# An RWKV-6 attention and its squared-ReLU MoE: new orders, DMA transposes for 12 chunks, the first four chunks in pairs

## The chip, the cores and the metric

The kernel runs on one core of one Trainium2 chip. The metric is device time in microseconds (us). The time before is the median of 3 runs, 212.34 us (211.41 to 213.89).

## What is computed

A linear attention with a decaying state, over 4 batches, 8 heads, 768 steps and a head dimension of 48, followed by a layer of the form ReLU squared on 3072 tokens of 384 values with 2048 hidden values:

```python
for t in range(S):                      # per batch b and head h, S = 768
    kt, vt, rt, wt = k[:, :, t], v[:, :, t], r[:, :, t], w[:, :, t]
    cur = einsum('bhd,bhe->bhde', u[None] * kt, vt)
    y[:, :, t] = einsum('bhd,bhde->bhe', rt, state + cur)
    state = wt[:, :, :, None] * state + einsum('bhd,bhe->bhde', kt, vt)
x = y.transpose(0, 2, 1, 3).reshape(B * S, H * D)      # 3072 x 384
h = maximum(x @ w_in, 0)                               # w_in 384 x 2048
out = (h * h) @ w_out                                  # w_out 2048 x 384
```

Inputs and output are float32; products are made in bfloat16.

## The kernel before

**Attention by chunks.** The steps are cut into chunks of 128: 6 chunks in each of 4 batches, 24 chunks s = 0 to 23 (`NSTEP`). A chunk has its 128 time steps in the partitions, and all 8 heads side by side (384 values). Four loads bring it (w, r, k, v; `load_one`, L71). In memory each (head, step) row has 48 floats, so a load of 192 KB consists of 1024 pieces of 192 bytes. Then, in the names of the code:

- `lw_` takes the logarithm of w (ACT). `cum_` multiplies it on TensorE by a strict upper triangle and by a negative inclusive one (L180, L181), which gives the running sums before and, negated, after each step; four one-column products (L178) give the sum over the whole chunk. `exp_` takes the exponentials (ACT), and `rd_` multiplies r and k with them (VectorE). The result, `rdec`, has each head padded to 64 columns.
- `tr_` transposes `rdec` by 8 TensorE products and `rkt_` copies them out of PSUM (VectorE). From chunk 18 on (`DMA_FROM`), `dtr_` does both by a transposing DMA (L208).
- `p_` multiplies decayed k and r (L223), `pm_` masks the product with the triangle, in two halves (L229).
- `su_` forms k times v (L238), `ts_` adds the old state, and `sn_` decays it to the next state (GpSimd).
- `y_` forms masked product times v (L260) and, except in a batch's first chunk, adds r times old state (L268).
- The u part needs no TensorE: `ku_`, `qp_` (GpSimd), `q_` (sum over each head, VectorE) and `vq_` (times v, GpSimd). `ysb_` adds it to y (VectorE).
- `yt_` transposes y by three TensorE products and `xt_` copies it (ACT) into `xT`, the MoE's input. From chunk 18 on `dyt_` does it by a transposing DMA (L213).

**MoE by blocks.** A block is one or two chunks (`blocks`). `m1_` multiplies xT with w_in (L301) into PSUM, 512 values wide; `rl_` is the ReLU (ACT, L308), `gt_` the square (VectorE, L313), `m2_` the product with w_out (L320), `os_` the scaled copy out (ACT) and `store` the output DMA (L329). w_in and w_out come in four loads of 768 KB each and are cast to bfloat16 on ACT and VectorE (L110).

**The order.** Each operation is put in a plan with its engine, an assumed duration, a rank, and what it depends on. `make_order` runs a list schedule over it, and the result is the order of instructions in each engine's queue; all queues run in order. Where TensorE would idle ahead of the first `m2_`, multiplies of zeros are put in (`warm_`, L334). All DMAs are issued from SP's queue. The loads' order there is fixed:

```python
seq = [(0, x) for x in "wrkvu"] + [(1, x) for x in "wrkv"] + [(g, "i") for g in range(4)]
seq += [(2, x) for x in "wrkv"] + [(g, "o") for g in range(4)]
seq += [(s, x) for s in range(3, NSTEP) for x in "wrkv"]
```

A chunk's input buffers are seven deep (`A_IN`); stores have the first rank on SP, then `dtr_` and `dyt_`, then loads.

Of the kernel before, what the change touches and what calls it, by code (L numbers as in the profile page):

```python
# [9 lines left out]
FP32 = mybir.dt.float32  # L10
FP16 = mybir.dt.float16
# [4 lines left out]

@with_exitstack
def kernel(
# [12 lines left out]
    PSUM = bass.MemoryType.PSUM  # L31

# [9 lines left out]
    NSTEP = B * NCH  # L42
    GW = 512
    RS = 16.0
    A_IN = 7
    HOP = .2
    PACE = 0.0
    DMA_FROM = 18
    LAG = 3.5

    nc.scalar.preload_act_table_set("natural_log_exp_and_others")

    consts = ctx.enter_context(tc.tile_pool(name="consts", bufs=1))
    weights = ctx.enter_context(tc.tile_pool(name="weights", bufs=1))
    stage_pool = ctx.enter_context(tc.tile_pool(name="stage", bufs=8))
    a_in = ctx.enter_context(tc.tile_pool(name="a_in", bufs=A_IN))
    a_mid = ctx.enter_context(tc.tile_pool(name="a_mid", bufs=2))
    a_small = ctx.enter_context(tc.tile_pool(name="a_small", bufs=3))
    gt_pool = ctx.enter_context(tc.tile_pool(name="gt", bufs=3))
    relu_pool = ctx.enter_context(tc.tile_pool(name="relu", bufs=3))  # L60
    o_pool = ctx.enter_context(tc.tile_pool(name="moe_out", bufs=3))

    ps_cp = ctx.enter_context(tc.tile_pool(name="ps_cp", bufs=1, space=PSUM))
    ps_y_pool = ctx.enter_context(tc.tile_pool(name="ps_y", bufs=1, space=PSUM))
    ps_tr_pool = ctx.enter_context(tc.tile_pool(name="ps_tr", bufs=1, space=PSUM))
    ps_m1 = ctx.enter_context(tc.tile_pool(name="ps_m1", bufs=2, space=PSUM))
    ps_m2 = ctx.enter_context(tc.tile_pool(name="ps_m2", bufs=1, space=PSUM))


    def load_one(dst, src, b, c):  # L70
        nc.sync.dma_start(  # L71
            out=dst, in_=src[b, :, c * C:(c + 1) * C, :].rearrange("h c d -> c h d"))

    raw = {}

    def load_step(step, part):
        b, c = divmod(step, NCH)
        if part == "w":
            raw["w", step] = a_in.tile([C, H, D], FP32, name="w_raw")
            load_one(raw["w", step][:], w, b, c)  # L80
        elif part == "r":
            raw["rk", step] = a_in.tile([C, 2, H, D], FP32, name="rk_raw")
            load_one(raw["rk", step][:, 0], r, b, c)
        elif part == "k":
            load_one(raw["rk", step][:, 1], k, b, c)
        else:
            raw["v", step] = a_in.tile([C, H, D], FP32, name="v_raw")
            load_one(raw["v", step][:], v, b, c)

    wi_sb = weights.tile([C, KT, DFF], BF16)  # L90
    wo_sb = weights.tile([C, NT, DM], BF16)
    xT = weights.tile([C, KT, B * S], BF16)
    w_st = {}

    def load_wi(g):
        w_st["i", g] = stage_pool.tile([C, KT, GW], FP32, name="w_st")
        nc.sync.dma_start(  # L97
            out=w_st["i", g][:],
            in_=moe_w_in[:, g * GW:(g + 1) * GW].rearrange("(a p) f -> p a f", p=128))

    def load_wo(g):
        w_st["o", g] = stage_pool.tile([C, 4, DM], FP32, name="w_st")
        nc.sync.dma_start(
            out=w_st["o", g][:],
            in_=moe_w_out[g * 512:(g + 1) * 512, :].rearrange("(a p) d -> p a d", p=128))

    def cast(eng, kind, g, j):
        dst = wi_sb[:, :, g * GW:(g + 1) * GW] if kind == "i" else wo_sb[:, g * 4:(g + 1) * 4, :]
        copy = nc.scalar.copy if eng == "A" else nc.vector.tensor_copy
        copy(dst[:, j], w_st[kind, g][:, j])  # L110

    u_bc = consts.tile([C, H, D], FP32)

    def load_u():
        nc.sync.dma_start(
            out=u_bc[:],
            in_=bass.AP(tensor=u.tensor, offset=u.offset,
                        ap=[[0, C]] + [list(x) for x in u.ap]))


    tri_strict = consts.tile([C, C], BF16)
    make_upper_triangular(nc, tri_strict[:], val=1.0, diag=False)
    tri_incl_neg = consts.tile([C, C], BF16)
    make_upper_triangular(nc, tri_incl_neg[:], val=-1.0, diag=True)
    ident = consts.tile([C, C], BF16)
    make_identity(nc, ident[:])
    ones_col = consts.tile([C, 1], BF16)
    nc.vector.memset(ones_col[:], 1.0)

    warm = consts.tile([C, 512], BF16)  # L130
    nc.vector.memset(warm[:], 0.0)  # L131

    NLW = 3
    lw_bufs = []
    for i in range(NLW):
        t = consts.tile([C, H, DP], BF16, name=f"lw_buf{i}")
        nc.gpsimd.memset(t[:], 0.0)
        lw_bufs.append(t)
    NRD = 3
    rdec_bufs = []  # L140
    for i in range(NRD):
        t = consts.tile([C, 2, H, DP], BF16, name=f"rdec_buf{i}")
        nc.vector.memset(t[:], 0.0)
        rdec_bufs.append(t)


    tiles = {}

    def lw_(s):
        lw = tiles["lw", s] = lw_bufs[s % NLW]  # L150
        nc.scalar.activation(lw[:, :, 0:D], raw["w", s][:], AF.Ln)  # L151

    def v_(s):
        v_bf = tiles["v", s] = a_mid.tile([C, H, D], BF16, name="v_bf", bufs=3)
        nc.scalar.copy(v_bf[:], raw["v", s][:])  # L155

    def ku_(s):
        ku = tiles["ku", s] = a_mid.tile([C, H, D], FP32, name="ku")
        nc.gpsimd.tensor_mul(ku[:], raw["rk", s][:, 1], u_bc[:])  # L159

    def qp_(s):
        qp = tiles["qp", s] = a_mid.tile([C, H, D], FP32, name="qprod")
        nc.gpsimd.tensor_mul(qp[:], raw["rk", s][:, 0], tiles.pop(("ku", s))[:])  # L163

    def q_(s):
        q = tiles["q", s] = a_small.tile([C, H], FP32, name="q")
        nc.vector.reduce_sum(q[:], tiles.pop(("qp", s))[:], axis=AX.X)  # L167

    def vq_(s):
        vq = tiles["vq", s] = a_mid.tile([C, H, D], FP32, name="vq", bufs=3)  # L170
        nc.gpsimd.tensor_mul(vq[:], raw["v", s][:],  # L171
                             tiles.pop(("q", s))[:, :, None].to_broadcast([C, H, D]))

    def cum_(s):
        lw = tiles.pop(("lw", s))
        cs = tiles["cs", s] = ps_cp.tile([C, 2, 512], FP32, name="cp")
        for p in range(HP):
            nc.tensor.matmul(cs[:, 0, DM + p:DM + p + 1], lw[:, 2 * p:2 * p + 2, :],  # L178
                             ones_col[:], start=True, stop=True)
        nc.tensor.matmul(cs[:, 0, 0:DM], tri_strict[:], lw[:, :, 0:D], start=True, stop=True)  # L180
        nc.tensor.matmul(cs[:, 1, 0:DM], tri_incl_neg[:], lw[:, :, 0:D], start=True, stop=True)  # L181

    def exp_(s):
        cs = tiles["cs", s]
        a_c = tiles["a_c", s] = a_small.tile([C, HP], FP32, name="a_c")
        nc.scalar.activation(a_c[:], cs[:, 0, DM:DM + HP], AF.Exp)
        nc.scalar.activation(cs[:, :, 0:DM], cs[:, :, 0:DM], AF.Exp)  # L187

    def rd_(s):
        rdec = tiles["rdec", s] = rdec_bufs[s % NRD]  # L190
        nc.vector.tensor_mul(  # L191
            rdec[:, :, :, 0:D], raw["rk", s][:],
            tiles.pop(("cs", s))[:, :, 0:DM].rearrange("p a (h d) -> p a h d", h=H))

    def tr_(s):
        rdec = tiles["rdec", s]
        ps_tr = tiles["tr", s] = ps_tr_pool.tile([C, 2, HP, C], BF16, name="tr")
        for i in range(2):
            for p in range(HP):
                nc.tensor.transpose(ps_tr[:, i, p, :], rdec[:, i, 2 * p:2 * p + 2, :], ident[:])  # L200

    def rkt_(s):
        rkT = tiles["rkT", s] = a_mid.tile([C, 2, HP, C], BF16, name="rkT")
        nc.vector.tensor_copy(rkT[:], tiles.pop(("tr", s))[:])  # L204

    def dtr_(s):
        rkT = tiles["rkT", s] = a_mid.tile([C, 2, HP, C], BF16, name="rkT")
        nc.sync.dma_start_transpose(  # L208
            out=rkT[:].rearrange("p i a t -> p (i a) t"),
            in_=tiles["rdec", s][:].rearrange("t i h d -> t (i h d)"))  # L210

    def dyt_(s):
        nc.sync.dma_start_transpose(  # L213
            out=xT[:, :, s * C:(s + 1) * C],
            in_=tiles.pop(("ysb", s))[:].rearrange("p h d -> p (h d)"))

    def p_(s):
        rkT = tiles["rkT", s]
        ps_p = tiles["p", s] = ps_cp.tile([C, 2, 512], FP32, name="cp")
        for p in range(HP):  # L220
            for e in range(2):
                rows = slice(e * DP, (e + 1) * DP)
# [291 lines left out]
```

## Time and profile before

| what | value |
|---|---|
| median of 3 runs | 212.34 us |
| the profiled execution: time, span, mean TensorE clock granted | 213.79 us, 212.0 us, 0.992 |
| L301 (m1): 480 products of 256 columns, 192 of 128 | 77.2 us busy |
| L320 (m2): 384 products of 384 columns | 74.8 us busy |
| L334 (warm-up): 60 products of 512 columns | 16.8 us busy |
| ReLU, L308, 128 x 512 | 96 x 598 ns |
| square, L313, 128 x 512 | 96 x 562 ns (median 425) |
| masking, L229, 128 x 512 | 48 x 682 ns |
| exponential, L187, 128 x 768 | 24 x 797 ns |
| ku, qp, vq on GpSimd | 24 each, 1012, 1052, 889 ns |
| `sn_` on GpSimd, 128 x 192 | 20 x 552 ns |
| a chunk load of 192 KB, issue to landing | 4.2 us (3.0 to 11.2) |
| dtr, issue to landing | 6, 3.3 us (3.0 to 4.6) |
| dyt, issue to landing | 6, 2.3 us (2.3 to 2.6) |
| a store of 192 KB, issue to landing | 2.0 us (1.9 to 4.3) |
| DMA: 115984 packets of data, share of the 16 engines' span | 72.6% |

Five engines are listed: PE (TensorE's products), PEld (its weight loads, which lie beside the products), DVE (VectorE), ACT (ScalarE) and POOL (GpSimd). SP is the queue that issues DMAs. In the 40 slices each digit is the busy share in tenths; a slice is 5.3 us. A line in order of time gives start, length, engine, line, operation, output and input, and the number of instructions in it. TensorE's products overlap, so the mean duration of one is longer than the distance to the next.

### The profile page before, as it was taken

The page shows a single profiled execution, that of the slowest core. Times are in us where ns is not written, and L with a number is a line of the kernel's source. Part 1 is how long each engine was busy: PE and PEld are TensorE (multiplying, and loading weights), DVE is VectorE, ACT ScalarE, POOL GpSimd, SP SyncE. Part 2 cuts the span into 40 slices and gives each one's busy share as a digit, 9 for nine tenths or more (in the row PEclk, how much of TensorE's full clock was granted, in tenths as well). Part 3 has the DMA queues.
Part 4 walks back from the last instruction along what each step waited for, and adds up shares of the span by engine and source line. Part 5 has one row for each costly group of instructions (what it writes and reads, how often), then busy time and mean ns, then how long its engine had stood idle before and what let it go on. Part 6 is the DMA issues. An engine that isn't in the chain of part 4 may idle for free.

```text
span 212.0 us, 5530 instructions
## 1 busy us (share of the span) xinstructions
PE 194.2 (92%) x2162; PEld 138.1 (65%) x2166; DVE 147.3 (69%) x273; ACT 125.2 (59%) x249; POOL 83.5 (39%) x105
## 2 busy tenths in 40 slices
PE   7897997886999898989989999999999999999983
PEld 3354766554877665767767677777767777777751
DVE  3565795555799798979968999987786666533310
ACT  3353967644666667568477376787645753455530
POOL 5371320545655719747276376363712110000000
PEclk9999999999799999999999999999999999999999
DMA  7999899879975899599978978899444327111111
GB/s 129 202 324 340 200 383 219 170 160 192 181 152 117 174 163 195 107 200 167 178 166 160 204 165 159 155 205 150 101 107 108 62 63 108 56 40 37 39 46 68
DMA packets 116010, 32.61 MB, mean 154 GB/s; under 512 B 109200, under 2 KB 114448, under 8 KB 115984
## 3 DMA queue, kind: packets, MB, share of 16 engines
q1 hardware_dynamic: 115984, 32.25, 72.6%
q8 instruction: 17, 0.28, 0.6%
q14 instruction: 9, 0.07, 0.1%
HBM read 25.36 MB, written 4.72 MB: 142 GB/s over the span
## 4 chain that ended last, share of the span: by engine, by line
PE 44%; DMA 17%; SPq 12%; issue 8%; DVE 8%; POOL 5%; ACT 4%; DVEq 0%; POOLq 0%; ACTq 0%
PE m L320 18%; PE m L301 17%; SPq L71 9%; DMA v_raw<-in_v_dram 6%; DMA w_st<-in_moe_w_out_dram 4%; DMA w_raw<-in_w_dram 3%; DVE gt L313 3%; PE cp L223 2%; POOL qprod L163 2%; DMA rk_raw<-in_r_dram 2%; DVE pmT L229 2%; PE tr L200 2%; ACT o_sb L325 2%; DMA rk_raw<-in_k_dram 2%; SPq L97 1%
## 5 line engine op out<-in xcount | busy, mean ns | idle before, releaser
L301 PE MATMUL m<-xT,wi_sb 128*128 128x256 bf16 (+1 forms) x672 | 77.2, 260 | 3.6 <-ACT xT L286 2.5
L308 ACT ACTIVATE rl<-m 128x512 f16<-128x512 f32 x96 | 56.5, 598 | 39.9 <-PE m L301 39.0
L320 PE MATMUL m<-wo_sb,gt 128*128 128x384 bf16 x384 | 74.8, 326 | 1.8 <-ACT o_sb L325 0.8
L301 PEld LDWEIGHTS <-wi_sb 128*128 128x128 bf16 x672 | 59.0, 99 | 16.8 <-issue 4.7
L313 DVE TENSOR_TENSOR gt<-rl 128x512 bf16<-128x512 f16 x96 | 52.5, 562 | 19.7 <-ACT rl L308 19.5
L320 PEld LDWEIGHTS <-gt 128*128 128x128 bf16 x384 | 35.3, 98 | 20.7 <-DVE gt L313 1.5
L159 POOL TENSOR_TENSOR ku<-rk_raw,u_bc 128x384 f32<-128x384 f32 x24 | 24.3, 1012 | 45.7 <-DMA rk_raw<-in_k_dram 41.1
L229 DVE TENSOR_TENSOR pmT<-cp,tri_strict 128x512 bf16<-128x512 f32 x48 | 30.8, 682 | 4.6 <-PE cp L223 4.4
L191 DVE TENSOR_TENSOR rdec_buf<-rk_raw,cp 128x768 bf16<-128x768 f32 x24 | 22.8, 949 | 13.9 <-ACT cp L187 10.9
L171 POOL TENSOR_TENSOR vq<-v_raw,q 128x384 f32<-128x384 f32 x24 | 21.3, 889 | 15.6 <-DVE q L167 7.6
L163 POOL TENSOR_TENSOR qprod<-rk_raw,ku 128x384 f32<-128x384 f32 x24 | 25.3, 1052 | 1.1
L251 POOL TENSOR_TENSOR S<-t_state,a_c 128x192 bf16<-128x192 f32 x20 | 11.0, 552 | 24.5 <-DVE t_state L247 17.6
L187 ACT ACTIVATE cp<-cp 128x768 f32<-128x768 f32 x24 | 19.1, 797 | 1.0 <-DVE gt L313 0.2
L334 PE MATMUL m<-warm 128*128 128x512 bf16 x60 | 16.8, 409 | 1.3 <-DVE warm L131 1.2
L155 ACT CAST v_bf<-v_raw 128x384 bf16<-128x384 f32 x24 | 12.3, 510 | 9.6 <-DMA v_raw<-in_v_dram 9.2
L151 ACT ACTIVATE lw_buf<-w_raw 128x384 bf16<-128x384 f32 x24 | 12.5, 523 | 7.9 <-DMA w_raw<-in_w_dram 6.1
L167 DVE TENSOR_REDUCE q<-qprod 128x8 f32<-128x384 f32 x24 | 13.1, 546 | 5.3 <-POOL qprod L163 5.3
L325 ACT ACTIVATE o_sb<-m 128x384 f32<-128x384 f32 x24 | 11.8, 492 | 7.7 <-PE m L320 7.0
L274 DVE TENSOR_TENSOR y_sb<-vq,y 128x384 bf16<-128x384 f32 x24 | 13.1, 548 | 3.3 <-PE y L268 3.2
L204 DVE COPY rkT<-tr 128x1024 bf16<-128x1024 bf16 x18 | 12.3, 682 | 1.9 <-PE tr L200 1.9
L200 PE MATMUL tr<-ident,rdec_buf 128*128 128x128 bf16 x144 | 11.5, 225 | 1.2 <-DVE rdec_buf L191 1.0
L223 PE MATMUL cp<-rkT 64*128 64x128 bf16 x192 | 9.7, 221 | 2.1 <-DVE rdec_buf L191 1.9
(40 smaller groups left out, 136.1 us busy)
## 6 DMA issues: line engine op xcount, KB each, us to landing
w_raw<-in_w_dram SPq DMA_DIRECT2D x24, 192.0 KB, 4.3
rk_raw<-in_r_dram SPq DMA_DIRECT2D x24, 192.0 KB, 4.2
rk_raw<-in_k_dram SPq DMA_DIRECT2D x24, 192.0 KB, 4.2
v_raw<-in_v_dram SPq DMA_DIRECT2D x24, 192.0 KB, 4.1
out_dram<-o_sb SPq DMA_DIRECT2D x24, 192.0 KB, 2.0
w_st<-in_moe_w_in_dram SPq DMA_DIRECT2D x4, 768.0 KB, 8.2
w_st<-in_moe_w_out_dram SPq DMA_DIRECT2D x4, 768.0 KB, 8.2
u_bc<-in_u_dram SPq DMA_DIRECT2D x1, 192.0 KB, 4.3
```

The costliest lines, as they stand in the source:

```text
L71: nc.sync.dma_start(out=dst, in_=src[b, :, c * C:(c + 1) * C, :].rearrange("h c d -> c h d"))
L159: nc.gpsimd.tensor_mul(ku[:], raw["rk", s][:, 1], u_bc[:])
L163: nc.gpsimd.tensor_mul(qp[:], raw["rk", s][:, 0], tiles.pop(("ku", s))[:])
L171: nc.gpsimd.tensor_mul(vq[:], raw["v", s][:], tiles.pop(("q", s))[:, :, None].to_broadcast([C, H, D]))
L187: nc.scalar.activation(cs[:, :, 0:DM], cs[:, :, 0:DM], AF.Exp)
L191: nc.vector.tensor_mul(rdec[:, :, :, 0:D], raw["rk", s][:], tiles.pop(("cs", s))[:, :, 0:DM].rearrange("p a (h d) -> p a h d", h=H))
L229: nc.vector.tensor_mul(tiles["pmT", s][:, e], tiles["p", s][:, e].rearrange("p (a t) -> p a t", a=HP), tri_strict[:, None, :].to_broadcast ...
L301: nc.tensor.matmul(ps1[:, j, :], wi_sb[:, kk, n * 128:(n + 1) * 128], xT[:, kk, s0 * C:s0 * C + width], start=(kk == 0), stop=(kk == KT - 1))
L308: nc.scalar.activation(rl[:], tiles.pop(("m1", i, g))[:], AF.Relu, scale=RS)
L313: nc.vector.tensor_mul(tiles["gt", i][:, g * ng:(g + 1) * ng, :], rl[:], rl[:])
L320: nc.tensor.matmul(tiles["m2"][:], gt[:, n, mt * 128:(mt + 1) * 128], wo_sb[:, n, :], start=(n == 0), stop=(n == NT - 1))
L334: nc.tensor.matmul(ps[:], warm[:, 0:C], warm[:], start=True, stop=True)
```

## The change

The body is written anew. What it does:

- The order is no longer planned when the program is built. It is a list of 931 names, `ORDER`, written out, which gives each engine's queue its order; "@n" names the PSUM bank, "warm" the warm-up products (29 in place of 60).
- Chunks 0 to 3 are loaded as two pairs. A pair is 256 time steps of one batch; partition p holds steps 2p and 2p+1, so a row has 384 bytes, and a pair takes four loads of 384 KB. The pair's attention is done on both halves x (even and odd steps): running sums from two triangles in 64-row blocks (`Pcum`), products in 64-row blocks (`Pp`), masks (`Ppm`), and so on. `g` is the pair's first or second chunk, i.e. partitions 0 to 63 or 64 to 127.
- Other chunks, but for 4 and 5 (`TWO`): one triangle only. Both exponentials are taken from its sums, with one as the negative; as the inclusive sum is missing, k is multiplied with 1/w beforehand: `iw` (ACT) and `kd` (GpSimd). The four one-column products move from `cum` to `su`, and their exponentials to `am`.
- The state has both heads of a pair of heads in 96 columns, with the unwanted half set to zero by `am`; `su` and the state part of `y` have 4 products of 96 columns where 8 of 48 stood, and `ts` and `sn` have 384 columns where 192 stood.
- dtr and dyt for chunks 12 to 23 (18 to 23 before).
- All MoE blocks have two chunks. m1's unit is 1024 wide in two PSUM banks: 48 units of 12 products, with 48 ReLU and 48 squares. One masking instruction of 1024 in place of two of 512.
- Input buffers: 14 slots of one chunk (all four inputs); weights use slots first, each of one load. xT is a ring of 12 chunks.
- u is loaded as one row and spread over the partitions by a product (`ub`, `ubc`). w_out's rows come two to a partition. The last tile of the output is computed, copied and stored in two halves.

The core of the diff:

```diff
+SLOTS = """
+p0:0 p1:2 i0:4 i1:5 i2:6 i3:7 s4:8 o0:9 o1:10 o2:11 o3:12 s5:13 s6:0 s7:1 s8:2 s9:3 s10:4 s11:5 s12:6 s13:7 s14:8
...
+ORDER = """
+LPw0 LPk0 warm7@7 LPr0 Plw0.1 Plw0.0 LPv0 Pcum0.0@0 warm5@7 Pex0.0 LPw1 Lu Prd0.0 LPr1 Pcum0.1@0 Pv0.1 Ptr0.0@3 Pex0.1
+warm4@7 LPk1 Prkt0.0 Pv0.0 Prd0.1 Plw1.0 ub@2 Ptr0.1@3 LPv1 ubc warm1@7 Li2 Prkt0.1 Pku0.0 Psu0@2 Pp0.1@0 ts0 am0 Li1
+Pku0.1 Pp0.0@4 Ppm0.1 Psu1@3 Li0 warm4@7 sn0 am1 Ppm0.0 Lw4 Plw1.1 Pqp0.0 Pcum1.1@0 Pv1.0 ts1 Pqp0.1 Py0.1@2 Pq0.0
+Pex1.1 Py0.0@3 sn1 Prd1.1 ciA2.1 Pvq0.0 warm1@7 Pq0.1 Pcum1.0@0 ciA2.0 Pku1.0 Pysb0.0 ciA2.2 warm1@7 Lr4 Pex1.0
+Pyt0.0@3 warm3@7 Pvq0.1 Pxt0.0 Prd1.0 Pv1.1 Pku1.1 Ptr1.1@3 warm2@7 Pysb0.1 Pqp1.0 Prkt1.1 Li3 Pyt0.1@2 warm1@7 Pxt0.1
+Ptr1.0@3 ciV1.1 ciA0.2 Lk4 Pq1.0 Pqp1.1 Psu3@2 ciA0.0 Prkt1.0 Lo0 ma0.2@4 ciA0.1 Pvq1.0 Pq1.1 Lo1 lw4 am3 ciV1.2
...
+rl4.1 mb3.1.2 q14 v13 Lr16 ku13 su12@2 xt11 cum13@0 ma4.3@4 ts12 am12 vq14 ex13 dtr12 gt4.1 mb3.1.3 rl4.3 Lv18 rd13
+sn12 mb4.0.1 qp13 os3.1 ma5.0@4 Lv15 gt4.3 st3.1 su13@3 q13 ku16 rl5.0 p12@0 dtr13 ts13 mb4.0.2 pm12 vq13 am13 ma5.1@4
...
+PAIRS = 2
+TWO = [4, 5]
+XRING = 12
+NSLOT = 14
+BLOCKS = [(0, 2), (2, 2), (4, 2), (6, 2), (8, 2), (10, 2), (12, 2), (14, 2), (16, 2), (18, 2), (20, 2), (22, 2)]
...
+    def load_pair(x, j):
+        src, at = SRC[x]
+        b, c = divmod(2 * j, NCH)
+        nc.sync.dma_start(out=pair(j)[:, at].rearrange("p h s d -> p h (s d)"),
+                          in_=src[b, :, c * C:(c + 2) * C, :].rearrange("h (p s) d -> p h (s d)", s=2))
...
+    def iw(s):
+        nc.scalar.activation(single(s)[:, 0], buf(lw_b, s)[:, :, 0:D], AF.Exp, scale=-1.0)
+
+    def kd(s):
+        nc.gpsimd.tensor_mul(single(s)[:, 0], single(s)[:, 2], single(s)[:, 0])
...
+    def cum(s, bank):
+        if s in TWO:
...
+        else:
+            nc.tensor.matmul(ps[:, bank + 1, 0:DM], tri[:], buf(lw_b, s)[:, :, 0:D], start=True, stop=True)
...
+            nc.scalar.activation(ps[:, bank, 0:DM], ps[:, bank + 1, 0:DM], AF.Exp, scale=-1.0)
+            nc.scalar.activation(ps[:, bank + 1, 0:DM], ps[:, bank + 1, 0:DM], AF.Exp)
...
+    def dtr(s):
+        nc.sync.dma_start_transpose(out=rt1(s), in_=buf(rd_b, s)[:].rearrange("t i h d -> t (i h d)"))
...
+    def su(s, bank):
+        for a in range(HP):
+            nc.tensor.matmul(ps[:, bank, a * 96:a * 96 + 96], buf(rd_b, s)[:, 1 - ri(s), 2 * a:2 * a + 2, :],
+                             buf(v_b, s)[:, 2 * a:2 * a + 2, :], start=True, stop=True)
+        for a in range(HP):
+            nc.tensor.matmul(ps[:, bank, DM + a:DM + a + 1], buf(lw_b, s)[:, 2 * a:2 * a + 2, :],
+                             ones[:], start=True, stop=True)
...
+    def Pcum(j, x, bank):
+        t = [buf(lw_b, 2 * j + i)[:, :, 0:D] for i in range(2)]
+        for b, (one, two) in enumerate((((bds, bds), (nbdi, nbds)), ((bdi, bds), (nbdi, nbdi)))[x]):
+            nc.tensor.matmul(ps[:, bank + b, 0:DM], one[:], t[0], start=True, stop=False)
+            nc.tensor.matmul(ps[:, bank + b, 0:DM], two[:], t[1], start=False, stop=True)
...
+    def Pp(j, h, bank):
+        t = rt2(j)
+        for a in range(2):
+            for s in range(2):
+                for g in range(2):
+                    for e in range(2):
+                        rows, cols = slice(e * DP, (e + 1) * DP), slice(g * 64, g * 64 + 64)
+                        nc.tensor.matmul(ps[cols, bank + e, (2 * a + s) * C:(2 * a + s + 1) * C],
+                                         t[rows, s, HP + 2 * h + a, cols], t[rows, :, 2 * h + a, cols],
+                                         start=True, stop=True)
...
+    def Py(j, x, bank):
+
+        nc.tensor.matmul(ps[:, bank, 0:DM], warm[:, 0:C], warm[:, 0:DM], start=True, stop=False,
+                         skip_group_check=True)
...
+                    nc.tensor.matmul(ps[cols, bank, a * 96:a * 96 + 96], rt2(j)[:, x, a, cols],
+                                     buf(st_b, s)[:, a * 96:a * 96 + 96], start=False, stop=False,
...
+            for s in range(2):
+                for rows in halves:
+                    nc.tensor.matmul(ps[rows, bank, h * D:(h + 1) * D], t[rows, e, a % 2, s, x * 64:x * 64 + 64],
+                                     buf(v_b, 2 * j + s)[rows, h, :], start=False, stop=s == 1,
...
+        for token in ORDER.split():
```

## The prediction

> **What bounds the kernel now.** I read the page's shares and slices first, then TensorE in order of time, then the chain of waits, then the DMA queue. The page:
>
> ```profile
> span 212.0 us, 5530 instructions
> PE 194.2 (92%) x2162; PEld 138.1 (65%) x2166; DVE 147.3 (69%) x273; ACT 125.2 (59%) x249; POOL 83.5 (39%) x105
> PE   7897997886999898989989999999999999999983
> DMA  7999899879975899599978978899444327111111
> ```
>
> TensorE looks full, but 60 of its instructions are warm-up multiplies and its ends are modelled, so I price it by the distance from one group's start to the next. TensorE in order of time, an undisturbed stretch:
>
> ```profile
> 121.72 0.36 PE L260 MATMUL y<-v_bf,pmT 128*128 128x48 bf16 x8
> ...
> 122.22 0.34 PE L283 MATMUL tr<-ident,y_sb 128*128 128x128 bf16 x3
> 122.40 0.24 PE L178 MATMUL cp<-ones_col,lw_buf 128*128 128x1 bf16 x4
> 122.50 0.32 PE L180 MATMUL cp<-lw_buf,tri_strict 128*128 128x384 bf16 x1
> ...
> 122.83 0.82 PE L301 MATMUL m<-xT,wi_sb 128*128 128x256 bf16 x6
> ...
> 126.28 0.61 PE L200 MATMUL tr<-ident,rdec_buf 128*128 128x128 bf16 x8
> 126.72 0.24 PE L178 MATMUL cp<-ones_col,lw_buf 128*128 128x1 bf16 x4
> ...
> 128.55 0.31 PE L238 MATMUL tr<-v_bf,rdec_buf 128*64 128x48 bf16 x8
> 128.79 0.82 PE L320 MATMUL m<-wo_sb,gt 128*128 128x384 bf16 x4
> ...
> 130.20 0.40 PE L223 MATMUL cp<-rkT 64*128 64x128 bf16 x8
> 130.53 0.62 PE L200 MATMUL tr<-ident,rdec_buf 128*128 128x128 bf16 x8
> ```
>
> So: y 0.50, yt 0.18, cum 0.43 (its four one-column products 0.10, each 384-column one 0.16), tr 0.44, su 0.24, p 0.33: 2.12 us a chunk, 1.50 without tr and yt. The end of the chain of waits is pure MoE:
>
> ```profile
> 191.40 1.31 PE m L301 x12
> 192.71 1.30 PE m L320 x8
> ```
>
> That is 0.109 us for 256 columns and 0.163 for 384: m1 is 480 x 0.109 + 192 x 0.055 = 62.9, m2 384 x 0.163 = 62.6. MoE 125.5 us; attention 24 x 1.50 + 18 x 0.62 less 1.8 (no old state in 4 chunks, no su in 4) = 45.4. Useful TensorE work: 171 us. It starts at 1.2 and its last product ends at 208.6, so **36.4 us of 207.4 are warm-up or idle**. Where? Adding up the groups that TensorE had begun by 57.5 us gives m1 of 4 chunks, m2 of 3 (18.3) and about 12 of attention: 30.3 useful in 56.3, 26 lost. After that only 10.4 of 151 are lost. The loss is in the ramp, and there the chain is SP's queue and DMA.
>
> ```profile
> 49.60 1.01 SPq L71 DMA_DIRECT2D rk_raw<-in_r_dram  x1
> 50.66 0.95 SPq L71 DMA_DIRECT2D rk_raw<-in_k_dram  x1
> ...
> 142.20 2.13 SPq L208 DMA_TRANSPOSE rkT<-rdec_buf  x1
> ...
> 153.07 1.18 SPq L213 DMA_TRANSPOSE xT<-y_sb  x1
> ```
>
> With the rings full, SP issues a load each 0.98 us (192 KB, 200 GB/s): the pace of 192-byte rows, 3.9 us a chunk. An issued transpose holds SP for 1.2 us, or 2.1 behind loads. In the ramp MoE has chunks 0 and 1, then waits: chunk 2's loads are queued behind all of w_in (3 MB), and chunk 3's behind w_out; chunk 3 is there at about 38 us.
>
> **TensorE's work, part by part.** Single chunks 6 to 23: one triangle product goes (-0.16); su's 96-column products cost 4 x 0.045 + the moved 0.10 = 0.28 against 0.24 + 0.10; y loses four small ones (-0.02). With the moved 0.10 counted once that is -0.25 by 18 chunks, -0.09 by chunks 4 and 5: -4.7. Six more chunks transposed by DMA: 6 x 0.62 = -3.7. Pairs add, with no such form in the trace: bounds are the nearest rows, 0.025 (64-row state product), 0.041 (p) and 0.056 (tr). A pair: Pcum 8 x 0.16 = 1.3; Ptr 0.9; Pp 32 x 0.041 to 0.056 = 1.3 to 1.8; Psu 2 x (8 x 0.037 to 0.056 + 0.2) = 1.0 to 1.3; Py 2 x (0.16 + 8 x 0.037 to 0.056 + 32 x 0.025 to 0.037) = 2.5 to 3.6; Pyt 0.4. In all 7.4 to 9.3 against 4.2 now; two pairs +6.4 to +10.2, middle 8, as the small ones resemble both rows. **Sum: 171 - 4.7 - 3.7 + 8 = about 170.6. TensorE's work hardly changes**, so whatever is won comes out of the 36.4.
>
> **The ramp.** Ahead of the first MoE come 8 pair loads of 384-byte rows. If a packet keeps its time, one pair load costs 0.98; if a byte does, 1.97. Weight loads with 2048-byte rows moved at 364 to 404 GB/s (8 to 24 us), so a packet of 192 bytes pays mostly a fixed price; at that rate 393 KB takes 1.05, which I take. Eight then cost 8.4 (bounds 7.9 to 15.8) against sixteen single ones, 15.7; u shrinks from 192 KB to one row (-1). The Trainium skill, "DMA: Bandwidth & Descriptors", section "Why small descriptors are slow", speaks against so much: about 3 cycles a packet beside one per 32 bytes, and by an estimate from it 15 cycles for 384 bytes against 9 for 192, so 1.63 a pair load and 13 us for eight; the trace's 200 GB/s at 192 bytes is itself lower than that rule's 6/9 of the ceiling, and no run here shows 384.
>
> Then in the new order, from 1.8: pairs to 10.2, Li2, Li1, Li0 (2.05 each) to 16.4, w4, r4, Li3 to 20.4, k4, Lo0, Lo1 to 25.5, v4, Lo3, Lo2 to 30.6, chunk 5 to 34.6; the landing comes some 2 us later. First m1 needs pair 0's xT. GpSimd sets it: u at about 7, then ku and qp of both halves (4 x 1.03), a ku of pair 1 (1.0), two sn and two vq (4 x 0.89) and some hops, to about 16.5; then ysb, yt, xt: 19 (21.2 now). In the written order TensorE has 11 us of useful work ahead of this: 7 lost. First m2 at about 30, as now, for w_out's casts: 2 to 3 more. From here four chunks of MoE (20.9) lie ready while chunks 4 and 5 come, so ramp loss is **11** where 26 stood; bounds 8, and 19 if packets cost by the byte.
>
> **After the ramp.** MoE and a single chunk cost TensorE 5.23 + 1.25, DMA 3.9 + store 0.55: TensorE is the bound. From chunk 12 DMA adds dtr and dyt. Between 152 and 168 us DMA was busy 33.6% (5.4 us) for 3 of each and 2 stores: 1.4 to 1.8 a chunk. So 6.1 of DMA against 6.5: nearly level. The loss now is 10.4; I take 9, as the smoother supply and the transposes pull apart; bounds 3 and 33 (below). Tail after the last product: 3.4 now; the last tile's copy and store are halved, 2.9.
>
> **Engines beside it.** ACT: iw +18 x 0.52, exp in two +3.6, am +3, relu over 1024 (0.598 + 512 x 0.75 ns = 0.98) 48 times for 96 x 0.598: -10, xt -2.9: 128 us. DVE: one pm of 1.2 for two of 0.68, rkT -4, ts +4, gt between 33 and 52: 130 to 147. GpSimd: kd +18 x 1.0, sn +20 x 0.34, masks +3: 112. All are under TensorE's 170 and hidden by MoE; kd stands before rd, so it lengthens a chunk's way by about 1.5 us, covered while the queues hold two MoE blocks; bare, it would be 18 x 1.5 = 27. SP: +12 transposes x 1.2 = 14.4 more.
>
> **Sum.** 1.2 + 170.6 + 11 + 9 + 2.9 = 194.7 span. The profiled execution was 213.79 with a span of 212.0, 1.45 above the median, so span + 0.3: **195**, range of this case 189 to 200.
>
> **Rivals.**
> *Smooth order (20%).* The order is written out, so idle time after the ramp could fall to 3 and ramp loss to 8: 186. For it: from 160 us on TensorE has next to no gaps now. Against: those had no loads beside them.
> *DMA and SP bound (20%).* By w22's issue DMA has moved 8.4 + 16.5 + 79 (20 chunks) + 16 stores, 8.8 + 10 chunks' transposes, 17, from 1.8: 131.5. At the use now (122.6 of such work in 152 us, 0.81) this is 162, and behind it stand about 31 us of TensorE's order, a landing of 4 and the tail 3: 200.
> *Transposes stall TensorE (18%), ending slower.* TensorE runs in order; SP too, and loads, stores and transposes share its queue. Between dtr and p the new order leaves 2.9 to 5.9 us of TensorE work (median 3.7), between a block's second dyt and its m1 only 2.0 to 5.8. Landing is 3.3 and 2.3 on a quiet queue, 4.6 for the one dtr behind loads. If loads are always ahead, add SP's 1: 5.6, so 12 x 1.9, and 6 blocks x 1.7: 33 in place of 9, 219. It decides from 2.2 us a chunk on. Against: loads wait behind the transposes in the same queue, which drains it.
> The change does what it says, since the order is fixed when the program is built.
>
> **Chances.** My case 42%. A measurement tells 1% from no change (210.2 to 214.5). Of the transpose case 4 fall within it, 14 above: faster 0.82, same 0.04, slower 0.14. Range 182 to 208: leaves out most of the third rival (0.16) and 0.04 below.
>
> **What would show it.** Right: the first m1 product near 19 us; DMA slices of 9 in the ramp; pair loads issued every 1.05 us; a TensorE idle sum by 57 us near 11 with warm-up; dtr landing under 4.6. Wrong: p or m1 waiting on the transposes for over 1 us each; GpSimd or VectorE ahead of p in the waits; SP waiting long on rd or ysb with loads behind it and DMA slices under 7 between 80 and 150 us; pair loads at 1.6 or more.

## The result and the profile after

| | before | after |
|---|---|---|
| median of 4 runs, us | 213.12 (211.41 to 214.7) | 194.0 (193.8 to 195.29) |
| the profiled execution: time, span, us | 213.79, 212.0 | 193.97, 192.2 |

The ratio is 0.914, with a 95% interval of 0.9057 to 0.9223: faster, by about 8.6%. The forecast was 195 us, in a range of 182 to 208.

The page of the kernel after, with the shares of the engines and the slices of TensorE and DMA:

```profile
span 192.2 us, 5027 instructions
PE 180.4 (94%) x1977; PEld 130.1 (68%) x1977; DVE 142.3 (74%) x203; ACT 126.6 (66%) x249; POOL 112.0 (58%) x136
PE   6799987889899999999999999999999999999993
DMA  6999799962989599797975897988989997522112
```

The share of TensorE hardly rose, though 20 us of span are gone; GpSimd's rose by 28 us of work. DMA now stays mostly at 7 to 9 until 160 us: its share is 0.82 to 1.00 in windows of about 20 us from 57 us on, where it was 0.65 from 140 to 160 us before.

To see where the 20 us came from, both executions are counted in one way. Every group of products gets a fixed price, read from the distances between group starts (384 columns 0.163 us, 256 0.109, 192 0.082, 128 0.056 or in 64-row form 0.041, 96 0.042, 48 0.026, one column 0.026; before the change 48 columns cost 0.030 in su and 0.037 in the masked half of y; in the pairs 128 columns in 64 x 64 form 0.018, 48 0.019, 96 columns 0.044 in Psu and 0.048 in Py, one column 0.034, and the product of zeros that opens a Py 0.256; u's two products 0.85; warm-up 0). What is left between the first product and the end of the last is lost; products at a lower clock count as loss too.

| us | before | after | forecast |
|---|---|---|---|
| to the first product | 1.2 | 1.2 | 1.2 |
| useful TensorE work | 171.0 | 166.0 | 170.6 |
| lost up to 57.5 us | 26.0 | 15.9 | 11 |
| lost after 57.5 us | 10.3 | 6.1 | 9 |
| after the last product | 3.4 | 3.0 | 2.9 |
| span | 212.0 | 192.2 | 194.7 |

So the gain is 5.0 of work, 10.1 of the ramp, 4.3 of the stretch after it, and 0.4 of the tail. Some 1.6 of the ramp's part is the clock: in the profile before, the granted clock was 0.50 from 52.0 to 55.4 us, and by the fixed prices the products there took 1.6 us longer; the changed kernel's ramp has no such stretch.

The work first. TensorE in order of time, from pair 0's attention and from chunk 5's:

```profile
12.24 0.64 PE L452 MATMUL ps<-rt 64*64 64x128 bf16 x32
12.82 0.51 PE L468 MATMUL ps<-v,rd 64*128 64x96 bf16 x8
...
14.98 0.33 PE L479 MATMUL ps<-warm 128*128 128x384 bf16 x1
15.23 0.36 PE L486 MATMUL ps<-st,rt 128*64 128x96 bf16 x4
15.52 0.69 PE L494 MATMUL ps<-v,pm 64*64 64x48 bf16 x32
16.14 0.34 PE L479 MATMUL ps<-warm 128*128 128x384 bf16 x1
...
49.14 0.37 PE L368 MATMUL ps<-v,pm 128*128 128x48 bf16 x8
49.35 0.33 PE L372 MATMUL ps<-st,rt 128*128 128x96 bf16 x4
49.52 0.33 PE L292 MATMUL ps<-lw,tri 128*128 128x384 bf16 x1
```

Reading start to start, Pp's 32 products take 0.58 us (both halves), Py 1.16, and a single chunk's y 0.38 where it took 0.50.

The ramp, from the same view:

```profile
22.45 1.49 PE L517 MATMUL ps<-xT,wi_sb 128*128 128x256 bf16 x12
...
29.86 1.48 PE L517 MATMUL ps<-xT,wi_sb 128*128 128x256 bf16 x12 [1.44 <-DVE wi_sb L243]
...
38.54 1.46 PE L543 MATMUL ps<-wo_sb,gt 128*128 128x384 bf16 x8 [0.60 <-DVE wo_sb L248]
40.75 0.37 PE L368 MATMUL ps<-v,pm 128*128 128x48 bf16 x8 [0.75 <-DVE pm L333]
```

The brackets hold the idle time ahead of a group and who ended it. The first MoE product comes at 22.45 us (21.22 before), later than before the change, but with 10.1 us of useful work done ahead of it and not 4.0. Ahead of it 11.1 us are lost (16.0 before), from there to 57.5 us 4.8 (10.0 before). In that second part TensorE has four holes, of 0.49 to 1.44 us; three of them are closed by VectorE, one by ACT, none by DMA.

The transposes, from the list of DMA issues (count, median us to landing) and from the answers on who waited for dtr and for dyt (us, times):

```profile
rt<-rd SPq DMA_TRANSPOSE x12, 3.2
xT<-ys SPq DMA_TRANSPOSE x12, 3.1
```

```profile
  PEld L327: 0.3, 1
```

```profile
  PEld L517: 0.6, 1
  PE ps L517: 0.2, 1
```

TensorE waited under half a microsecond for the twelve dtr and under one for the twelve dyt.

### The profile page after: what moved, and what is told of

Same layout as the page of the kernel before. It is cut to its first block, busy times and chain, and to the rows that moved or that the text cites. A ratio compares the mean times of both kernels' runs of the same rounds, so it can differ in the third digit from the quotient of the medians.

```text
span 192.2 us, 5027 instructions
## 1 busy us (share of the span) xinstructions
PE 180.4 (94%) x1977; PEld 130.1 (68%) x1977; DVE 142.3 (74%) x203; ACT 126.6 (66%) x249; POOL 112.0 (58%) x136
## 4 chain that ended last, share of the span: by engine, by line
PE 56%; DVE 15%; DMA 9%; ACT 8%; issue 5%; POOL 3%; SPq 2%; DVEq 0%; ACTq 0%; POOLq 0%
PE ps L543 24%; PE ps L517 20%; DMA raw<-in_w_dram 6%; DMA raw<-in_v_dram 2%; ACT rl L524 2%; DVE pm L459 2%; PE ps L327 2%; DVE pm L333 2%; PE ps L368 2%; DVE wi_sb L243 2%; DVE wo_sb L248 2%; PE ps L313 1%; DVE ts L357 1%; DVE rt L317 1%; DVE q L277 1%
## 5 line engine op out<-in xcount | busy, mean ns | idle before, releaser
L517 PE MATMUL ps<-xT,wi_sb 128*128 128x256 bf16 x576 | 70.5, 273 | 2.0 <-DVE wi_sb L243 1.4
L543 PE MATMUL ps<-wo_sb,gt 128*128 128x384 bf16 (+1 forms) x400 | 71.3, 320 | 1.1 <-DVE wo_sb L248 0.6
L524 ACT ACTIVATE rl<-ps 128x1024 f16<-128x1024 f32 x48 | 49.1, 1022 | 33.3 <-PE ps L517 33.1
L528 DVE TENSOR_TENSOR gt<-rl 128x1024 bf16<-128x1024 f16 x48 | 42.3, 884 | 14.4 <-ACT rl L524 14.3
L265 POOL TENSOR_TENSOR raw<-raw 128x384 f32<-128x384 f32 x18 | 19.4, 1076 | 13.3 <-ACT raw L262 8.6
L280 POOL TENSOR_TENSOR vq<-raw,q 128x384 f32<-128x384 f32 x20 | 17.8, 893 | 15.7 <-DVE q L277 12.4
L333 DVE TENSOR_TENSOR pm<-ps,tri 128x1024 bf16<-128x1024 f32 x20 | 24.3, 1217 | 2.2 <-PE ps L327 2.2
L274 POOL TENSOR_TENSOR qp<-raw,qp 128x384 f32<-128x384 f32 x20 | 21.9, 1101 | 3.6 <-DMA raw<-in_r_dram 3.4
L271 POOL TENSOR_TENSOR qp<-raw,u_bc 128x384 f32<-128x384 f32 x20 | 21.9, 1094 | 3.7 <-DMA raw<-in_k_dram 3.1
L305 DVE TENSOR_TENSOR rd<-raw,ps 128x768 bf16<-128x768 f32 x20 | 19.0, 949 | 4.7 <-ACT ps L301 2.9
L259 ACT ACTIVATE lw<-raw 128x384 bf16<-128x384 f32 x20 | 10.4, 522 | 4.2 <-DMA raw<-in_w_dram 4.1
L268 ACT CAST v<-raw 128x384 bf16<-128x384 f32 x20 | 10.1, 510 | 0.5 <-DMA raw<-in_v_dram 0.5
```

Source lines behind the costliest of these rows:

```text
L265: nc.gpsimd.tensor_mul(single(s)[:, 0], single(s)[:, 2], single(s)[:, 0])
L271: nc.gpsimd.tensor_mul(buf(qp_b, s)[:], single(s)[:, 2], u_bc[:])
L274: nc.gpsimd.tensor_mul(buf(qp_b, s)[:], single(s)[:, 1], buf(qp_b, s)[:])
L280: nc.gpsimd.tensor_mul(vq_b[:, s % BUFS["vq"]].rearrange("p (h d) -> p h d", h=H), single(s)[:, 3], buf(q_b, s)[:, :, None].to_broadcast([ ...
L305: nc.vector.tensor_mul(buf(rd_b, s)[:, :, :, 0:D], single(s)[:, x:x + 2], ps[:, bank:bank + 2, 0:DM].rearrange("p a (h d) -> p a h d", h=H))
L333: nc.vector.tensor_mul(buf(pm_b, s)[:].rearrange("p e a t -> p (e a) t"), ps[:, bank:bank + 2].rearrange("p e (a t) -> p (e a) t", t=C), t ...
```

## The experiments

All times are medians; the kernel before was run beside each on the same chip, and since its median moved between 213.1 and 215.1 us from run to run, the ratios are what is to be compared. "Lost" is counted as in the table above.

**The halved packets alone.** The pair loads are cut in two:

```diff
-        nc.sync.dma_start(out=pair(j)[:, at].rearrange("p h s d -> p h (s d)"),
-                          in_=src[b, :, c * C:(c + 2) * C, :].rearrange("h (p s) d -> p h (s d)", s=2))
+        for s in range(2):
+            nc.sync.dma_start(out=pair(j)[:, at, :, s],
+                              in_=src[b, :, c * C:(c + 2) * C, :].rearrange("h (p s) d -> p h s d", s=2)[:, :, s])
```

> Each of the eight pair loads is split into two DMAs, one for even and one for odd steps, so the rows are 192 bytes again; layout, order and everything else stay. Theory (the ramp is set by what DMA has to bring): 16 loads at 0.98 us in place of 8 at 1.15 put all weights and chunk 4 back by 6.5 us, and the time goes from 194.0 to 199 to 200.5. Rival (the pairs' way through GpSimd, which started at 11.55 us, and VectorE, full from 24 to 32 us, sets the ramp): DMA has slack there and the time moves by 0 to 2 us.

Measured: 198.6 us, ratio 0.9265 (0.9196 to 0.9334), 0.0125 above the first run of the changed kernel, 2.7 us (3.7 above its second run, below). The profiled span is 197.2, 5.0 longer, and the loss up to 57.5 us is 20.3 for 15.9. SP's queue in order of time, first the changed kernel, then this one:

```profile
6.77 1.15 SPq L214 DMA_DIRECT2D raw<-in_k_dram  x1
...
9.15 2.27 SPq L218 DMA_DIRECT2D raw<-in_moe_w_in_dram  x3
```

```profile
11.45 1.84 SPq L215 DMA_DIRECT2D raw<-in_k_dram  x2
...
15.54 2.66 SPq L219 DMA_DIRECT2D raw<-in_moe_w_in_dram  x3
```

w_in is issued 6.4 us later, as the theory said, and 2.7 (by ratio) to 5.0 us (by span) of it reach the end. That is between the two theories: by span near the first, by ratio near the second. The extra loss lies ahead of the first m1 product, which comes at 27.30 us: 16.0 us are lost there for 11.1, and 4.4 for 4.8 behind it. A part of it may be the clock, which was 0.50 from 14.2 to 17.6 us in this profile. So the halved packets give between a quarter and nearly half of the ramp's gain.

**Six chunks back on TensorE.** dtr and dyt of chunks 12 to 17 give way to `tr rkt` and `yt xt`, one product group later in the order:

```diff
-... dtr12 gt4.1 mb3.1.3 rl4.3 ...
+... gt4.1 mb3.1.3 tr12@2 rkt12 rl4.3 ...
```

> Chunks 12 to 17 are transposed on TensorE again (tr, rkt, yt, xt in the places of dtr and dyt, one large product later); chunks 18 to 23 stay with DMA. Theory (TensorE's order is the bound after the ramp): 6 x 0.62 us more on TensorE, 197.5 to 198. Rival (DMA and SP hold the middle, where the chain of waits shows loads of w between 112 and 129 us): 12 transposes fewer free 14 us of SP and 10 of DMA, and the time is 192 to 194.

Measured: 202.15 us, ratio 0.9426 (0.9355 to 0.9498), some 6 to 7 us slower than the changed kernel, more than either theory gave. Useful work rose by 3.7, as priced; 4.5 us more were lost, all after 57.5 us. One of the new holes, in TensorE's order:

```profile
122.23 0.36 PE L368 MATMUL ps<-v,pm 128*128 128x48 bf16 x8 [0.50 <-DVE rt L317]
```

The hole is at VectorE's copy out of PSUM. The rival is out. But the extra loss may belong to my places for the products in a written order as much as to the transposes; the run does not tell them apart.

**Both triangles everywhere.**

```diff
-TWO = [4, 5]
+TWO = list(range(4, 24))
```

and all `iw` and `kd` leave the order.

> Every single chunk takes both triangles (as chunks 4 and 5 do), and iw and kd are left out: 18 more products of 384 columns on TensorE, 18 x 1.08 us less on GpSimd, about 18 x 0.65 less on ACT. Theory (TensorE bound): 18 x 0.16 = +2.9, 196.5 to 197. Rival (the longer way through ACT and GpSimd costs as much as it saves): 193 to 194.5.

Measured: 194.82 us, ratio 0.9089 (0.9028 to 0.915): no slower. Useful work is 168.9, 2.9 more, as priced; but the loss after 57.5 us falls to 3.0 from 6.1 (5.3 in the second profile of the changed kernel). The one-triangle form saves TensorE's work and gives nearly all of it back in lost time.

**The transposes alone, in the old kernel.**

```diff
-    DMA_FROM = 18
+    DMA_FROM = 12
```

> The kernel before with DMA_FROM = 12: only the six more chunks transposed by DMA, in its own planned order. Theory (TensorE bound after 57 us): -3.7 us, 209 to 210. Rival (the transposes stand on SP among the loads and come late): 213 or more.

Measured: 222.16 us, ratio 1.0292 (1.0168 to 1.0415): slower, by 1.7 to 4.2%. Useful work fell to 167.3, but 22.4 us are lost after 57.5 (10.3 before). TensorE's order in the worst place:

```profile
108.23 0.81 PE L301 MATMUL m<-xT,wi_sb 128*128 128x256 bf16 x6 [1.80 <-ACT rl L308]
110.52 0.61 PE L223 MATMUL cp<-rkT 64*128 64x128 bf16 x8 [1.48 <-DVE rdec_buf L191]
```

SP's queue ahead of it, and ACT:

```profile
95.78 0.94 SPq L71 DMA_DIRECT2D v_raw<-in_v_dram  x1
100.44 1.34 SPq L208 DMA_TRANSPOSE rkT<-rdec_buf  x1
101.87 0.52 SPq L329 DMA_DIRECT2D out_dram<-o_sb  x1
102.44 0.53 SPq L71 DMA_DIRECT2D w_raw<-in_w_dram  x1
```

```profile
107.17 0.52 ACT L151 ACTIVATE lw_buf<-w_raw 128x384 bf16<-128x384 f32 x1 [5.80 <-DMA w_raw<-in_w_dram]
107.60 0.58 ACT L308 ACTIVATE rl<-m 128x512 f16<-128x512 f32 x1
```

Read backwards: m1 waits for rl; rl stands behind lw on ACT; lw waited 5.8 us for a w that SP issued only at 102.44, since SP had stood from 96.7 to 100.44 at a dtr whose rd was not yet made (VectorE wrote it from 99.47 to 100.41). The hole ahead of p is the same delay one step on: p needs the PSUM that rd reads, and rd runs from 109.51, after the lw, Pcum and exponential that were late. So TensorE does not wait for a dtr to land (the views name no wait for one in this run); in this place it waits for loads that stand behind a dtr. From 57.5 to 175 us, the waits of ACT for w and v from DRAM add up to 26.6 us here:

```profile
ACT lw_buf L151 <- DMA w_raw<-in_w_dram: 24.1, 10, 5.8
...
ACT v_bf L155 <- DMA v_raw<-in_v_dram: 2.5, 3, 1.3
```

(total, times, longest; the wait view from 57 us). Before they were 6.4, in the changed kernel 4.6 and 2.4 in its second profile.

The granted clock falls as well: its slices show 5 of 10 from 110 to 116 us, after these holes, and 6 in two other slices, one of them in the ramp. By the fixed prices the products at half clock after 57.5 us make some 4 of the 22.4 us lost. In the changed kernel every slice has 9.

**The changed kernel again**, beside the next three.

> The changed kernel as it is, so that the others of this call stand beside it on one chip: 0.914 of the kernel before, within its interval.

Measured: 194.03 us, ratio 0.9093 (0.904 to 0.9145). Its ramp lost 16.8 us, for 15.9 in the first profile. The difference lies ahead of the first m1 product, which comes at 23.40 us, not 22.45: TensorE ran at half its pace for longer at the start. The first running sums (Pcum), in the first profile and in this one:

```profile
5.42 0.32 PE L420 MATMUL ps<-lw,bds 128*128 128x384 bf16 x1
5.58 0.32 PE L419 MATMUL ps<-lw,nbdi 128*128 128x384 bf16 x1
```

```profile
5.48 0.52 PE L420 MATMUL ps<-lw,bds 128*128 128x384 bf16 x1
5.80 0.52 PE L419 MATMUL ps<-lw,nbdi 128*128 128x384 bf16 x1
```

They come 0.16 us apart there and 0.32 here; from about 9.2 us on it is 0.16 here too. The profiles fall into two groups by this. With the full pace from the first Pcum on, m1 begins at 22.45 to 22.54 us (the first profile, x2, and v4 and v6 below); with half pace until 9 to 10 us, at 23.40 to 24.20 (this one, x3, and v1, v2, v3 and x4 below). So the start of m1 is to be compared within a group.

**u first.** `Lu` goes second on SP, `ub` and `ubc` ahead of the first `Pcum` and `Pex`; ku, qp, q, vq of pair 0 ahead of `sn`:

```diff
-LPw0 LPk0 warm7@7 LPr0 Plw0.1 Plw0.0 LPv0 Pcum0.0@0 warm5@7 Pex0.0 LPw1 Lu ...
+LPw0 Lu LPk0 warm7@7 LPr0 Plw0.1 Plw0.0 LPv0 ub@2 Pcum0.0@0 warm5@7 ubc Pku0.0 Pku0.1 Pex0.0 LPw1 ...
```

> u's row is loaded second instead of sixth, ub and ubc come ahead of the first Pcum and Pex, and ku, qp, q, vq of pair 0 move ahead of the state's sn on GpSimd and VectorE. Theory (the ramp loss was under-priced because GpSimd began at 11.55 us and not at 7): GpSimd starts at about 6, the first m1 product comes near 20 instead of 22.45, and the time falls by 1.5 to 2.5 us. Rival (the weights' landing and casts set the ramp from 25 us on): within 0.5 us of the changed kernel.

Measured: 194.67 us, ratio 0.9135 (0.9095 to 0.9174): no gain. GpSimd's line and the first m1 product of this run:

```profile
6.75 0.99 POOL L403 TENSOR_TENSOR qp<-raw,u_bc 128x384 f32<-128x384 f32 x1 [1.83 <-ACT u_bc L255]
```

```profile
24.20 1.48 PE L517 MATMUL ps<-xT,wi_sb 128*128 128x256 bf16 x12
```

GpSimd started 4.8 us earlier than in the first profile, and m1 did not: of the runs that begin at half pace, as this one does, those without this edit start m1 at 23.40 to 24.02 us. GpSimd is not what set the start.

**Contiguous casts.**

```diff
-        copy(wi_sb[:, kk, 4 * g:4 * g + 4].rearrange("c (n j) p -> c n j p", j=2),
-             weight(f"i{g}", KT)[:, kk].rearrange("c (n p j) -> c n j p", p=128, j=2))
+        copy(wi_sb[:, kk, 4 * g:4 * g + 4].rearrange("c n p -> c (n p)"), weight(f"i{g}", KT)[:, kk])
...
+                          in_=moe_w_out[g * 512:(g + 1) * 512, :].rearrange("(n p) d -> p n d", p=128))
```

> The casts of w_in are contiguous and w_out's rows lie one to a partition (1536-byte pieces) as in the kernel before. Theory (VectorE is full from 24 to 32 us and its strided w_in casts of 0.80 us hold m1 back by 1.4 us at 28.4): casts fall to 0.42, 2.3 us of VectorE come free there, the time falls by 1 to 2 us. Rival (VectorE's time is shared with GpSimd, not the stride; or w_out's smaller pieces come later): within 0.5 us or slower.

Measured: 193.87 us, ratio 0.9106 (0.9057 to 0.9154): no change. The cast's group, here and in the changed kernel:

```profile
L243 DVE CAST wi_sb<-raw 128x512 bf16<-128x512 f32 x6 | 4.6, 800 | 0.0
```

```profile
L243 DVE CAST wi_sb<-raw 128x512 bf16<-128x512 f32 x6 | 4.6, 801 | 0.0
```

The stride costs nothing. The same cast took 422 ns before the change.

**Both of these.** The two edits above together.

> Both of the last two together. Theory (two separate holds in the ramp): the sum, 2.5 to 4 us faster than the changed kernel, 190 to 191.5 on the chip of the first runs. Rival (one hides the other): no better than the better of the two.

Measured: 194.75 us, ratio 0.9135 (0.9092 to 0.9178). The sum of two nothings.

**Sixteen chunks by DMA.** Chunks 8 to 11 too, with dtr behind rd and dyt behind ysb:

```diff
-... rd9 ... tr9@3 ... rkt9 ... p9@4 ... ysb9 ... yt9@2 xt9 ...
+... rd9 dtr9 ... p9@4 ... ysb9 dyt9 ...
```

> The changed kernel with chunks 8 to 11 transposed by DMA too: 16 chunks, dtr right behind rd and dyt right behind ysb in SP's order, leaving 2.9 to 5.0 us of TensorE work to p and 4.0 to 11.7 to m1. Theory 1 (TensorE's sum decides wherever the slack covers the landing): 4 x 0.62 = 2.5 us faster, ratio to the kernel before 0.90. Theory 2 (what decides is how far the loads are ahead on SP's queue; at chunk 8 they are one or two chunks ahead, at chunk 12 four): SP stands before rd with loads behind it, and the time grows by 2 us or more, ratio 0.92 or above.

Measured: 203.65 us, ratio 0.9494 (0.9432 to 0.9557): some 8 us slower, though useful work fell by 2.5. The loss after 57.5 us is 16.5, most of it before 100 us; some 1.5 of it comes from products at a granted clock of 0.50, from 81.2 to 84.6 us. In TensorE's order dtr now ends holes itself:

```profile
69.10 0.40 PE L327 MATMUL ps<-rt 64*128 64x128 bf16 x8 [1.27 <-DMA rt<-rd]
...
93.11 0.40 PE L327 MATMUL ps<-rt 64*128 64x128 bf16 x8 [0.67 <-DMA rt<-rd]
```

The time follows theory 2, but how far the loads are ahead, counted in issues, does not explain it. On SP's queue, when dtr of chunk 8 went out, loads of 0.8 chunk beyond chunk 8 had been issued; for chunks 9 to 11 it is 1.8, 2.0 and 1.8. In the changed kernel this lead is 3.0 chunks at chunk 12, falls to 1.0 at chunk 18 and 0.3 at chunk 19, with hardly a hole; in the old kernel with 12 transposes it was 2.0 to 2.3 at chunks 12 to 17, with many. The lead does not sort the fast kernels from the slow. What does, among these three, is how long ACT waits for w and v to land, counted as for the old kernel with twelve transposes: 15.2 us here, against 4.6 and 2.4 in the changed kernel.

```profile
ACT lw L259 <- DMA raw<-in_w_dram: 10.6, 10, 3.2
ACT v L268 <- DMA raw<-in_v_dram: 4.6, 5, 1.6
```

Three of the largest holes end at ACT soon after such a wait (80.84 us, 1.50 for v; 97.54, 1.35 and 104.78, 1.42 for rl). The first of the waits, 3.24 us, follows SP's stand ahead of dtr of chunk 8, from 60.9 to 64.47 us.

**Stores on ACT's queue.**

```diff
-        nc.sync.dma_start(out=dst, in_=o)
+        nc.scalar.dma_start(out=dst, in_=o)
```

> The stores are issued from ACT's queue instead of SP's, right behind the copy they wait for; all else stays. Theory 2 (in-order waits on SP hold loads back): SP loses 33 us of waits for os, loads land earlier, idle after the ramp falls from 6 to about 4, the time by 1 to 2 us. Theory 1 (TensorE's sum): those waits are covered, and 25 issues cost ACT some 10 us of its 65 free: 0 to +1 us.

Measured: 193.52 us, ratio 0.904 (0.8978 to 0.9103); the profiled span is 191.3. That is up to a microsecond less than the changed kernel, but the intervals overlap: not shown.

**The order of loads alone, in the old kernel.**

```diff
-    seq += [(2, x) for x in "wrkv"] + [(g, "o") for g in range(4)]
-    seq += [(s, x) for s in range(3, NSTEP) for x in "wrkv"]
+    seq += [(s, x) for s in (2, 3) for x in "wrkv"] + [(g, "o") for g in range(4)]
+    seq += [(s, x) for s in range(4, NSTEP) for x in "wrkv"]
```

> The kernel before with one change in the order of its loads: chunk 3 comes ahead of w_out. Theory (the ramp's loss of 26 us comes from chunks 2 and 3 behind the weights, so order alone wins part of it): 2 to 4 us faster than the kernel before. Rival (the first m2 goes back by 4 us and DMA has the same to bring until 57 us): within 1 us or slower; then it is the halved packets and not the order that shortened the ramp.

Measured: 214.33 us, ratio 1.0005 (0.9965 to 1.0044): nothing. The loss is 22.9 by 40 us (20.0 before), 23.8 by 57.5 (26.0), and 12.0 after that (10.3). Each profile has one stretch at a granted clock of 0.50 that makes some 1.6 us, from 52.0 to 55.4 us before and from 70.9 to 74.4 us here; without it 24.4 and 10.3 stand against 23.8 and 10.4. Hardly anything is won.

**A version meant to beat both.** On top of the stores on ACT, VectorE's order between 28 and 41 us is changed:

```diff
-... ciV3.2 ciV3.1 ex4 ciV3.0 ... coV1.3 q4 ... rkt4 ... ts4 coV3.3 coV1.0 ... coV3.1 ... pm4 ... coV3.0
+... ciA3.0 ... ciV3.2 ciV3.1 ex4 ... coV1.3 coV1.0 q4 ... rkt4 ... ts4 ... pm4 coV3.3 coV3.1 ... coV3.0
```

> Stores from ACT's queue as in v4_store_act, and on VectorE, between 28 and 41 us, the cast of w_out's second group and chunk 4's pm come ahead of the fourth group's casts, and one w_in cast of the fourth group goes to ACT. The changed kernel's TensorE has three holds there: 1.44 us for the w_in cast, 0.60 for the w_out cast, 0.75 for pm. Theory (these are VectorE's order, in a stretch where it is full): about 2 us of them go, the loss by 57 us falls from 15.8 to 14, the time to 191 or a little below, ratio 0.895. Rival (the same VectorE work only holds something later): ratio 0.90 to 0.91 as without.

Measured: 193.82 us, ratio 0.9022 (0.8951 to 0.9092). The three holes are nearly gone, and others stand a few microseconds on:

```profile
41.33 0.34 PE L385 MATMUL ps<-ident,ys 128*128 128x128 bf16 x3 [1.09 <-DVE ys L378]
...
42.47 2.77 PE L543 MATMUL ps<-wo_sb,gt 128*128 128x384 bf16 x16 [0.47 <-DVE gt L528]
```

The loss is 12.4 by 40 us (14.1 in the changed kernel) and 15.4 by 57.5 (15.9): the rival's story. It beats the kernel before, and is not told apart from the changed kernel.

## Why the prediction was right, and where its terms were off

**Direction and size.** The main step held: TensorE's work changes by little, and what is won comes out of its lost time, most of it in the ramp. Useful work fell by 5.0 us, lost time by 14.4. That the total came within 1 us (195 against 194.0) owes something to terms that cancel: work 4.6 below its forecast, the ramp's loss 4.9 above, the stretch after it 2.9 below. Of the signs named for being right, the first m1 product near 19 us and a ramp loss near 11 failed; dtr landed within 4.6 us but for the slowest, at 4.8.

**TensorE's work (forecast 170.6, 166.0 measured).** The pairs were mis-sized. A pair was put at 7.4 to 9.3 us; it took about 6.7 (Pcum 1.3, Ptr 0.9, Pp 0.6, Psu 1.2, Py 2.3, Pyt 0.35), below the low end. The nearest rows gave 0.041 and 0.025 us for the small products; those in 64 x 64 form cost 0.018 and 0.019. And y was said to lose 0.02 a chunk; it lost 0.12.

**The ramp (forecast 11, 15.9 measured, within the bounds of 8 and 19).** The pair loads were sized nearly right: SP issues one each 1.15 us where 1.05 was taken. (The 364 to 404 GB/s behind the 1.05 were read a little narrowly: in slices of 0.4 us from 14 to 19 us, with weight loads alone, the trace has 348 to 405.) Between 3 and 11 us, with pair loads and u's row alone, DMA moved 312 to 326 GB/s, 1.2 us for 393 KB. The rule of the Trainium skill that was weighed ("DMA: Bandwidth & Descriptors", "Why small descriptors are slow") gave 1.63 by an estimate; here the measurement decides, and 384-byte rows are cheaper than that. The step that failed is "GpSimd sets it: ... 19": GpSimd began at 11.55 us and not at 7, because `ub` stands behind the running sums, warm-up and a group of transposes in TensorE's order, and m1 came at 22.45; but starting GpSimd at 6.75 moved nothing. In the chain of waits the stretch from 12 to 30 us is mostly VectorE's:

```profile
12.88 1.05 DVE pm L459
14.01 1.22 DVE pm L459
...
19.21 0.95 DVE rd L431
20.55 0.69 DVE rt L317
...
22.12 0.68 DVE rt L317
...
23.26 1.39 DVE wi_sb L243 x2
...
25.70 1.21 DVE pm L459
...
28.59 1.22 DVE wi_sb L243
```

VectorE was priced as a whole, at 130 to 147 us, and said to be hidden. It took 142 of 192, but from 24 to 32 us it is busy without a gap, and the last run (v6_casts_order) shows that its order there only moves the holes. Between a quarter and nearly half of the ramp's gain of 10.1 is the halved packets (x1_rows192), and some 1.6 us is the low clock in the profile before; loads in another order win nothing in the old kernel (b2_chunks_first). What made the rest, I did not separate.

**After the ramp (forecast 9, 6.1 measured).** kd and iw were costed at nothing, covered by MoE. That was wrong by 2 to 3 us: without them the loss after the ramp is 3.0, for 6.1 and 5.3 with them (x3_two_products), which nearly pays for the 2.9 us of products that they save.

**The rivals.** "Smooth order" did not come true: 15.9 and 6.1 us were lost where it needs 8 and 3. "Transposes stall TensorE" did not come true in this order, but its sign is real, and its mechanism in part: the same twelve chunks by DMA make the old kernel 2.9% slower (1.7 to 4.2; b1_dma12, "b1" below), and four chunks more make the new one some 8 us slower (x4_dma8, "x4"). Its price was put at 2.2 us a chunk to decide; in x4 the loss after 57.5 us grows by 2.6 for each of the four. But the place was wrong: the cost is less in TensorE's wait for a transpose (x4 has four such holes, 2.6 us in all) than in the loads that stand behind a waiting transpose on SP, and in ACT, which waits for them ahead of MoE's rl. The waits of ACT for loads go with the loss after 57.5 us where transposes were given to DMA: 6.4 and 10.3 us before, 26.6 and 22.4 in b1; 4.6 and 6.1 in the changed kernel, 15.2 and 16.5 in x4. They are not the only source of loss: x2, with fewer transposes by DMA, waits 0.7 us and loses 10.6. This is read from the traces, not shown; loads or transposes on another queue, which would test it, were not tried. Nor is it settled which part of the written order keeps SP from standing long at a dtr in chunks 12 to 23. The DMA rival was near: DMA's share is 0.82 to 1.00 from 57 to 160 us.

## What to carry to other kernels

Count the useful work of the bound engine apart from its busy time, and split what is lost by stage: a rewrite whose work falls by only 5 us can still win another 14 out of lost time, most of it in the ramp. Moving work off the bound engine pays only where the waits it brings are covered: the same twelve DMA transposes were harmless in one order, while in another, where loads stood behind waiting transposes and came late, the kernel was 2.9% slower. On a queue that serves in order, price what stands behind the waiting step. A fully busy stretch of an engine that is idle a quarter of the time overall is where an order, or a hidden step, has to be priced.

## What was unexpected of the hardware

- Products in 64 x 64 form, four to the array, cost 0.018 us for 128 columns each; full ones 0.056, those of 64 rows 0.041.
- The VectorE cast of 128 x 512 from float32 took 0.42 us before and 0.41 to 1.21 us, 0.80 in the mean, in the changed kernel, and not for its stride (801 ns strided, 800 contiguous). In the run with both ramp edits the one that fell into a GpSimd pause took 0.42; where GpSimd was busy beside it for 0.6 of its time it took 0.42 too, and where it was busy for over 0.7, up to 1.21. That GpSimd is the cause was not tried.
- A transposing DMA among loads: dyt lands in 3.1 us (2.3 to 4.8) where it took 2.3 on a quieter queue, and its issue held SP for up to 3.35 us where 1.20 is the median.
- Rows of 384 bytes move at 312 to 326 GB/s, those of 192 bytes at about 200 (194 to 214 in x1).
- The granted clock fell to 0.50 for 3.4 us without a long hole ahead of it: at 52.0 us in the kernel before, where the longest hole of the 10 us ahead was 0.79 us; at 81.2 us in x4 after one of 1.50 us. And the changed kernel came to its full pace ahead of 5.3 us in one execution, and at 9.2 us in another.
